# Loading 128 tokens' rows for all channels with one transfer, and the next head's v one slot later

## The chip, the cores and the metric

The kernel runs on one core of one Trainium2 chip. The metric is the device time of one execution in microseconds (us), taken as the median of several runs. A profile of one further execution (the profiled execution) shows each instruction of each engine: PE (matrix multiplications; PEld is its loading of weights), DVE (vector), ACT (activations), POOL (GpSimd) and SP, a queue that computes nothing and issues transfers (DMAs). In this kernel SP issues all of them, strictly in the order of the program: a transfer that has to wait for something holds up every later one.

## The reference

Causal attention with a decay over 8 batches x 8 heads of 576 tokens and 64 columns each, then a layer norm and a two-layer perceptron with a residual:

```python
B, H, S, D = q.shape                                   # 8, 8, 576, 64
scores = scale * np.matmul(q, k.transpose(0, 1, 3, 2))
cum = np.cumsum(np.log(np.clip(f, 0.0001, 1.0)), axis=-1)
scores = np.where(causal, -1000000000.0, scores + cum[:, :, :, None] - cum[:, :, None, :])
attn = np.exp(scores - np.max(scores, axis=-1, keepdims=True))
attn = attn / (np.sum(attn, axis=-1, keepdims=True) + 1e-09)
x = np.matmul(attn, v).transpose(0, 2, 1, 3).reshape(B, S, H * D)   # 8 x 576 x 512
mu, var = mean and variance of x over its last axis
xn = (x - mu) / np.sqrt(var + 1e-06) * g_ln
out = x + np.maximum(xn @ w_ch1, 0.0) @ w_ch2          # 512 -> 2048 -> 512
```

## The kernel before

**Heads and slots.** The 64 (batch, head) pairs are worked through one after the other. A head n has four query tiles t = 1 to 4 (a small tile 0 goes along with t = 1), and the program is a list of slots (n, t). The first 16 heads (`h.full`) run in one precision; from head 16 on (`NFULL`) operands are split in a high and a low part, and the scaled probabilities are carried from a tile `p` to a tile `pw` by a DMA (L440) before PE transposes them (L446). In slot (n, t) PE forms the scores (`qk_mm`, L376 and L377), DVE takes the maximum (L409), ACT the exponential (L420), DVE the reciprocal, POOL scales `p` (L427), and SP issues `pw<-p` (L440). The transposes of that tile are due two slots later (`LAG = 2`), the product with v (`av_unit`, L543) three slots later.

**The perceptron** takes chunks of 256 tokens and runs 16 steps per chunk (`FT`), one step in each slot as long as heads last, so that a chunk takes exactly four heads; what is left of it runs behind the last head. Before a chunk, its channels come back from DRAM (`xa`, `xb`: for each batch tokens 0 to 319 and 320 to 575) in four blocks of 128 channels, tiles `xr` (L655, `chunk_load`), which ACT and DVE split (L606, L607). For the layer norm's statistics and for the residual the same tokens are needed once more as rows: `rows_load` loads 128 tokens x 512 channels into a tile `xw`, again with channels on the partitions, and two steps later four PE transposes (`chunk_rows`, L446, `xp<-identr,xw`) turn it. `rows_load` runs in steps 9 and 11 of a chunk. In the part of the program where steps and slots go together, those are slots t = 1 and t = 3 of every fourth head, n = 17, 21, ..., 61.

**Order inside a slot.** A string of letters says which piece of which stage is written when. From slot 66 on it is

```python
    (66, "QSAFteahBlMPrmNbRLD"),
```

The letters that issue DMAs: `a` writes finished heads to `xa` or `xb` (L592), `B` issues `pw<-p`, `P` is `prep()` (a constant row `kl` at t = 2; the split of v, `prep_v`, at t = 3; `load_v` of the next head), `N` writes results, `R` loads `xw` and then `xr`, `D` loads a tile `raw` of q or k for the head after next (t = 2 and 3). Each engine works in the order in which the pieces are written. `prep_v` of head n reads the tile `vr` (DVE L356, then POOL L357), of which there is one buffer, so `load_v` of head n+1 (L332) has to wait for POOL L357 of head n.

**A wait behind each transfer.** Every DMA reports on one of eight semaphores, used in turn; a DMA also waits for the earlier one of its semaphore.

Of the kernel before, what the change touches and what calls it, by code (L numbers as in the profile page):

```python
# [8 lines left out]
F32 = mybir.dt.float32  # L9
# [6 lines left out]
B, H, S, D = 8, 8, 576, 64  # L16
DM, DFF = H * D, 4 * H * D
P = 128
KT = DM // P
FT = DFF // P  # L20
NTOK = B * S
C = 256
NCHUNK = NTOK // C
S1 = 320
# [4 lines left out]
LAG = 2  # L29
# [27 lines left out]
def attn_moe(ctx: ExitStack, tc: tile.TileContext, qk, v, f, g, w1, w2, out):  # L57
    nc = tc.nc
# [15 lines left out]
    def m2(name, dt):  # L74
        return work.tile([P, 512], dt, tag="m2", bufs=11, name=name)
# [8 lines left out]
    def busy(n):  # L84
# [9 lines left out]
        out=mask[:, S - P :], in_=mask[:, S - P :], pattern=[[-1, P]], base=0,  # L94
# [198 lines left out]
    xd1 = [dram.tile([DM, S1], F32, tag=f"xa{b}", name=f"xa{b}") for b in range(B)]  # L293
    xd2 = [dram.tile([DM, S - S1], F32, tag=f"xb{b}", name=f"xb{b}") for b in range(B)]
# [32 lines left out]
    def load_v(h):  # L327
        if h.full and h.n % 2 == 1:
            h.vr = work.tile([P, 5, 2, D], F32, tag="vv", bufs=1, name=f"vr{h.n}")[:, :, 0, :]
        else:  # L330
            h.vr = work.tile([P, 5, D], F32, tag="vr", bufs=1, name=f"vr{h.n}")
        nc.sync.dma_start(out=h.vr, in_=v[h.n])  # L332
# [28 lines left out]
    def qk_mm(h, t):  # L361
        q0, m, w = QT[t]
        cuts = [(0, w)] if w <= 512 else [(0, w // 2), (w // 2, w)]
        h.s = getattr(h, "s", {})
        h.s[t] = []
        if t == 0:
            w = P
            m = P if h.full else m
            cuts = [(0, w)]
        for i, (a, z) in enumerate(cuts):  # L370
            sp = bank(f"s{h.n}_{t}_{i}")[:m, : z - a]
            xq, kl = h.xq[:, q0 : q0 + m], h.kl[:, a:z]
            if h.full:
                mm(sp, xq, kl, start=True, stop=True)  # L374
            else:
                mm(sp, h.hi[:, 0, q0 : q0 + m], h.hi[:, 1, a:z], start=True, stop=False)  # L376
                mm(sp, xq, kl, start=False, stop=True)  # L377
            if t == 0:
                z, sp = a + QT[0][2], sp[: QT[0][1], : QT[0][2]]
            h.s[t].append((a, z, sp))  # L380
# [18 lines left out]
    def softmax_a(h, t):  # L399
        q0, m, w = QT[t]  # L400
        nm = f"{h.n}_{t}"
        if t == 0:
            pt = corner(h.n)
        else:
            pt = work.tile([P, S], F32, tag="p", bufs=3, name=f"p{nm}")
        st = work.tile([P, 4], F32, tag="st", bufs=6, name=f"st{nm}")
        off = S - P - (w - m)
        for i, (a, z, sp) in enumerate(h.s[t]):
            nc.vector.tensor_tensor_reduce(  # L409
                out=pt[:m, a:z], in0=sp, in1=mask[:m, off + a : off + z], scale=-SCALE,  # L410
                scalar=3.0e38 if i == 0 else st[:m, 0:1], op0=ALU.add, op1=ALU.min, accum_out=st[:m, i : i + 1],
            )
        h.p = getattr(h, "p", {})
        h.p[t] = (pt, st)

    def softmax_e(h, t):
        q0, m, w = QT[t]
        pt, st = h.p[t]
        i = len(h.s[t]) - 1
        nc.scalar.activation(pt[:m, :w], pt[:m, :w], AF.Exp, bias=st[:m, i : i + 1], scale=-1.0, accum_out=st[:m, 2:3])  # L420
# [81 lines left out]
    def transposed_hi(h, t):  # L502
        for tp, hi, lo in h.parts:
            nc.scalar.copy(out=hi, in_=tp)  # L504

    def transposed_lo(h):
        if not h.full:
            for tp, hi, lo in h.parts:
                nc.vector.tensor_tensor(out=lo, in0=tp, in1=hi.bitcast(F32), op=ALU.subtract)  # L509
# [129 lines left out]
    def mm2(c, j, h):  # L639
        if j == 0:  # L640
            c.acc = [ps.tile([P, DM], F32, tag=f"acc{i}", bufs=1, name=f"acc{c.n}_{i}") for i in range(2)]
        for i in range(2):
# [2 lines left out]
            mm(c.acc[i], h[:, 0, ts_], w2l[:, j, :], start=False, stop=False)  # L645
            mm(c.acc[i], h[:, 1, ts_], w2h[:, j, :], start=False, stop=(j == FT - 1))  # L646

    def tokens(c, k, t0, m, out_):

        t = t0  # L650
        while t < t0 + m:
            b, o = divmod(t, S)
            src, o0, lim = (xd1[b], 0, S1) if o < S1 else (xd2[b], S1, S)
            w = min(t0 + m - t, lim - o)
            nc.sync.dma_start(out=out_[:, t - t0 : t - t0 + w], in_=src[P * k : P * k + P, o - o0 : o - o0 + w])  # L655
            t += w

    def rows_load(c, i):
        c.xw = m2(f"xw{c.n}_{i}", F32R).rearrange("p (k c) -> p k c", k=KT)
        for k in range(KT):  # L660
            tokens(c, k, c.n * C + P * i, P, c.xw[:, k, :].bitcast(F32))

    def chunk_rows(c, i):

# [120 lines left out]
    hd = {}  # L785
# [14 lines left out]
    for u, slot in enumerate(slots):  # L800

        def before(k):
            return slots[u - k] if u >= k else None

        if slot is not None:
            n, t = slot
            h = hd[n]
        av = None
        if before(LAG + 1) is not None and before(LAG + 1)[1] in (2, 4):
            av = hd[before(LAG + 1)[0]]  # L810
        want = moe.can(wp.ready()) and u >= FIRST_MOE

        def piece(c):
            tu = before(LAG)
            if c == "t" and tu is not None:
                transpose_unit(hd[tu[0]], tu[1])
            elif c == "h" and tu is not None:
                transposed_hi(hd[tu[0]], tu[1])
            elif c == "l" and tu is not None:
                transposed_lo(hd[tu[0]])  # L820
            elif c == "Q" and slot is not None:
                if t == 1:
                    qk_mm(h, 0)
                qk_mm(h, t)
            elif c == "A" and av is not None:
                av_unit(av, before(LAG + 1)[1])
            elif c == "S" and slot is not None:
                if t == 1:
                    softmax_a(h, 0)
                softmax_a(h, t)  # L830
            elif c == "e" and slot is not None:
                if t == 1:
                    softmax_e(h, 0)
                softmax_e(h, t)
            elif c in FILL:
                wp.fill(FILL[c])
            elif c == "s":
                wp.sums()
                if u == LAG:
                    busy(WARM[2])  # L840
            elif c == "F" and av is not None:
                finish(av)
            elif c == "a" and av is not None:
                finish_add(av)
            elif c == "r" and want:
                moe.first_high()
            elif c == "R":
                moe.limit = min(NCHUNK, max(0, u - LAG - 1) // (4 * H) * S // C)
                moe.rest()
            elif c == "b":  # L850
                rows_stats(moe.cur)
            elif c == "L":
                run_later(RSTD)
            elif c == "M" and want:
                moe.first()
            elif c == "B" and slot is not None:
                if t == 1:
                    softmax_b(h, 0)
                softmax_b(h, t)
            elif c == "m" and want:  # L860
                moe.first_low()
            elif c == "W":
                due = 1 + min(u, W_CHANGE) / W_SLOTS + max(0, u - W_CHANGE) * W_TICKS
                while not wp.done() and wp.tick_no <= due:
                    wp.tick()
            elif c == "N":
                moe.second()
            elif c == "P":
                prep()
            elif c == "D":  # L870
                next_raw()

        def next_raw():

            if slot is not None and t in (2, 3) and NFULL <= n + 2 < B * H:
                if t == 2:
                    start_head(n + 2)
                load_raw(hd[n + 2], 1 if t == 2 else 0)

        def prep():  # L880

            if slot is not None:
                if t == 1 and n + 1 < NFULL:
                    start_head(n + 1)
                if n == NFULL - 2 and t == 1:
                    while not wp.done():
                        wp.tick()
                        wp.fill(99)
                    early.close()
                    pools["late"] = ctx.enter_context(tc.tile_pool(name="late", bufs=1))  # L890
                if n + 1 >= NFULL and n + 1 < B * H:
                    if t == 2:
                        prep_a(hd[n + 1])
                    if t == 3:
                        prep_b(hd[n + 1])
                if not h.full and t == LAG + 1:
                    prep_v(h)
                if t == LAG + 1 and n + 1 < B * H:
                    load_v(hd[n + 1])

        for c in [o for first, o in ORDERS if first <= u][-1]:
            piece(c)
# [48 lines left out]
```

## Time and profile before

| | |
|---|---|
| time, median of 3 runs | 1250.09 us (1249.48 to 1256.52) |
| profiled execution | 1250.83 us, its span from first to last instruction 1249.1 us |
| PE busy | 1197.9 us of the span, 96% |
| DVE, ACT, POOL busy | 749.0, 620.4, 452.4 us |
| DMA | 139.04 MB in 129657 packets, mean 111 GB/s |
| mean granted clock of PE | 0.990 |

Three stages follow each other: the full heads with the unpacking of the weights (to 223 us), the heads 16 to 63 with the perceptron's steps (223 to some 1030 us), and the rest of the perceptron (to 1249 us). Busy time counts instructions that compute. "Idle before, releaser" at a row is how long its engine had nothing to do, and what ended that.

### The profile page before, as it was taken

How to read it: one execution, taken by the hardware profiler on the slowest of the kernel's cores; microseconds unless marked ns; L12 is line 12 of the kernel's file. 1: busy time of each engine (PE TensorE's matmuls, PEld its weight loads, DVE VectorE, ACT ScalarE, POOL GpSimd, SP SyncE). 2: the span in 40 equal slices, each digit the busy share in tenths (PEclk: the TensorE clock that was granted, in tenths of full speed). 3: DMA queues.
4: the chain of work that ended last, by engine and by line, in shares of the span. 5: the costliest groups of instructions: out<-in, count | busy, mean ns of one | idle time of the engine just before them, and what ended most of it. 6: DMA issues, size and time to landing. Idle time of an engine off the chain costs nothing.

```text
span 1249.1 us, 26052 instructions
## 1 busy us (share of the span) xinstructions
PE 1197.9 (96%) x8368; PEld 1070.7 (86%) x8368; DVE 749.0 (60%) x2664; ACT 620.4 (50%) x1936; POOL 452.4 (36%) x768
## 2 busy tenths in 40 slices
PE   8888998999999999999999999998989999999998
PEld 6557887889898989899898989887989899999997
DVE  6777683466676767676666676766767662222222
ACT  6886574455555555555455555555545542112111
POOL 3544344344444434354434444444434330000000
PEclk9998998999999999999999999999999999999999
DMA  6554442244334343433433444433343421110100
GB/s 187 150 158 144 128 133 66 87 131 130 116 128 140 124 136 125 137 125 117 134 124 126 131 133 131 133 121 116 127 130 124 137 81 39 51 35 17 52 27 26
DMA packets 129657, 139.04 MB, mean 111 GB/s; under 512 B 34544, under 2 KB 102128, under 8 KB 129520
## 3 DMA queue, kind: packets, MB, share of 16 engines
q1 hardware_dynamic: 129520, 137.37, 35.6%
q8 instruction: 67, 1.10, 0.4%
q14 instruction: 70, 0.57, 0.2%
HBM read 79.61 MB, written 19.17 MB: 79 GB/s over the span
## 4 chain that ended last, share of the span: by engine, by line
PE 81%; DVE 6%; DMA 5%; ACT 4%; issue 2%; POOL 1%; SPq 1%; DVEq 0%; POOLq 0%; ACTq 0%
PE h L622 11%; PE h L624 10%; PE h L623 10%; PE acc L644 10%; PE acc L645 10%; PE acc L646 10%; PE o L543 5%; DMA pw<-p 4%; PE tr L446 4%; PE s L376 3%; PE s L377 3%; PE s L374 2%; PE o L518 2%; DVE p L409 2%; ACT p L420 2%
## 5 line engine op out<-in xcount | busy, mean ns | idle before, releaser
L427 POOL TENSOR_SCALAR p<-p,st 64x64 f32<-64x64 f32 (+4 forms) x320 | 169.7, 532 | 542.2 <-ACT ph L504 310.0
L622 PE MATMUL h<-x,w1h 128*128 128x256 f32 x1152 | 342.3, 297 | 5.7 <-DVE pl L509 5.3
L624 PE MATMUL h<-x,w1l 128*128 128x256 f32 x1152 | 326.8, 284 | 0.0
L623 PE MATMUL h<-x,w1h 128*128 128x256 f32 x1152 | 326.4, 283 | 0.0
L420 ACT ACTIVATE p<-p,st 64x64 f32<-64x64 f32 (+4 forms) x320 | 179.2, 560 | 229.0 <-DVE st L409 216.6
L635 DVE SCALAR_TENSOR_TENSOR hh<-h,hh 128x256 fp32r<-128x256 f32 x288 | 120.4, 418 | 194.9 <-ACT hh L630 194.8
L622 PEld LDWEIGHTS h<-x,w1h 128*128 128x128 f32 x1152 | 219.6, 191 | 11.0 <-issue 6.6
L644 PE MATMUL acc<-w2h,hh 128*128 128x512 f32 x576 | 228.9, 397 | 0.0
L645 PE MATMUL acc<-w2l,hh 128*128 128x512 f32 x576 | 228.3, 396 | 0.0
L646 PE MATMUL acc<-w2h,hh 128*128 128x512 f32 x576 | 225.9, 392 | 0.0
L623 PEld LDWEIGHTS h<-x,w1h 128*128 128x128 f32 x1152 | 220.9, 192 | 2.5
L624 PEld LDWEIGHTS h<-x,w1l 128*128 128x128 f32 x1152 | 220.6, 191 | 0.0
L630 ACT ACTIVATE hh<-h 128x256 fp32r<-128x256 f32 x288 | 109.9, 382 | 185.0 <-PE h L624 184.6
L409 DVE CUSTOM_DVE_ANT_0 p<-s,mask 64x64 f32<-64x64 f32 (+4 forms) x320 | 132.4, 422 | 43.8 <-DMA pw<-p 22.1
L646 PEld LDWEIGHTS acc<-w2h,hh 128*128 128x128 f32 x576 | 108.7, 189 | 25.0
L644 PEld LDWEIGHTS acc<-w2h,hh 128*128 128x128 f32 x576 | 109.9, 191 | 14.2 <-ACT ph_full L504 0.2
L425 DVE TENSOR_SCALAR st<-st 128x1 f32<-128x1 f32 (+1 forms) x320 | 47.5, 149 | 121.0 <-ACT p L420 118.2
L645 PEld LDWEIGHTS acc<-w2l,hh 128*128 128x128 f32 x576 | 109.8, 191 | 11.9
L504 ACT CAST ph<-tr 64x128 fp32r<-64x128 f32 (+4 forms) x384 | 107.2, 328 | 3.7 <-PE tr L446 1.4
L579 ACT COPY ot<-o 64x320 f32<-64x320 f32 x96 | 37.9, 395 | 119.3 <-PE tr L446 60.1
L446 PE MATMUL tr<-identr,pw 128*128 128x128 f32 (+1 forms) x672 | 79.4, 235 | 18.3 <-DMA pw<-p 18.2
L509 DVE TENSOR_TENSOR pl<-tr,ph 128x128 fp32r<-128x128 f32 x192 | 88.0, 458 | 4.4
(89 smaller groups left out, 1885.1 us busy)
## 6 DMA issues: line engine op xcount, KB each, us to landing
raw<-in_qk_dram SPq DMA_DIRECT2D x96, 288.0 KB, 2.9
wr<-in_w_dram SPq DMA_DIRECT2D x32, 512.0 KB, 5.9
pw<-p SPq DMA_DIRECT2D x48, 288.0 KB, 3.3
pw<-p SPq DMA_DIRECT2D x48, 224.0 KB, 2.2
vr<-in_v_dram SPq DMA_DIRECT2D x64, 160.0 KB, 2.3
out_dram<-xt SPq DMA_DIRECT2D x36, 256.0 KB, 2.1
pw<-p SPq DMA_DIRECT2D x48, 160.0 KB, 2.1
xa<-xs SPq DMA_DIRECT2D x32, 160.0 KB, 1.8
```

The source lines that it names most:

```text
L409: nc.vector.tensor_tensor_reduce(out=pt[:m, a:z], in0=sp, in1=mask[:m, off + a : off + z], scale=-SCALE, scalar=3.0e38 if i == 0 else st[: ...
L420: nc.scalar.activation(pt[:m, :w], pt[:m, :w], AF.Exp, bias=st[:m, i : i + 1], scale=-1.0, accum_out=st[:m, 2:3])
L427: nc.gpsimd.tensor_scalar(out=pt[:m, :w], in0=pt[:m, :w], scalar1=st[:m, 3:4], scalar2=1.0, op0=ALU.mult, op1=ALU.mult)
L446: nc.tensor.transpose(out_.bitcast(F32R), in_, identr[:m, :m])
L622: mm(ph, w1h[:, k, fs], c.x[k][:, 0, :], start=(k == 0), stop=False)
L623: mm(ph, w1h[:, k, fs], c.x[k][:, 1, :], start=False, stop=False)
L624: mm(ph, w1l[:, k, fs], c.x[k][:, 0, :], start=False, stop=(k == KT - 1))
L630: nc.scalar.activation(h[:, 0, :], c.ph, AF.Relu)
L635: nc.vector.scalar_tensor_tensor(out=h[:, 1, :], in0=ph, scalar=0.0, in1=h[:, 0, :].bitcast(F32), op0=ALU.max, op1=ALU.subtract)
L644: mm(c.acc[i], h[:, 0, ts_], w2h[:, j, :], start=(j == 0), stop=False)
L645: mm(c.acc[i], h[:, 0, ts_], w2l[:, j, :], start=False, stop=False)
L646: mm(c.acc[i], h[:, 1, ts_], w2h[:, j, :], start=False, stop=(j == FT - 1))
```

## The change

Two edits. `rows_load` issues one DMA for all four blocks of 128 channels instead of one DMA per block: the source is viewed as partition x block x token. Where the 128 tokens lie on both sides of a border between `xa` and `xb`, there are two such DMAs, in place of eight. In all, 44 DMAs write `xw` instead of 176. And for heads that aren't full, `load_v` of the next head is issued at t = 4 instead of t = 3.

```diff
+    def piece_of(t, end):
+        b, o = divmod(t, S)
+        src, o0, lim = (xd1[b], 0, S1) if o < S1 else (xd2[b], S1, S)
+        return src, o - o0, min(end - t, lim - o)
...
     def rows_load(c, i):
         c.xw = m2(f"xw{c.n}_{i}", F32R).rearrange("p (k c) -> p k c", k=KT)
-        for k in range(KT):
-            tokens(c, k, c.n * C + P * i, P, c.xw[:, k, :].bitcast(F32))
+        t = t0 = c.n * C + P * i
+        while t < t0 + P:
+            src, o, w = piece_of(t, t0 + P)
+            nc.sync.dma_start(
+                out=c.xw[:, :, t - t0 : t - t0 + w].bitcast(F32),
+                in_=src.rearrange("(k p) s -> p k s", p=P)[:, :, o : o + w],
+            )
+            t += w
...
-                if t == LAG + 1 and n + 1 < B * H:
+                if t == LAG + 1 and h.full and n + 1 < B * H:
+                    load_v(hd[n + 1])
+                if t == LAG + 2 and not h.full and n + 1 < B * H:
                     load_v(hd[n + 1])
```

`tokens`, which loads `xr`, uses `piece_of` too and does what it did. PE, DVE, ACT and POOL keep their instructions in their order; what moves is on SP.

The first place is SP around slot (17, 3). In a row, `pw17_3` is head 17's tile 3, `vr18` is v of head 18, `xw1_1` the second half of chunk 1's rows, `xr2_3` a block of chunk 2. Before:

```order
L440 DMA pw17_3_3249<-p17_3_3220 128x448
L332 DMA vr18_3272<-in_v_dram 128x320
L655 DMA xw1_1_3288<-xb0_155 128x128 x4
L655 DMA xr2_3_3293<-xb0_155 128x64
L655 DMA xr2_3_3293<-xa1_148 128x192
L325 DMA raw19_0_3296<-in_qk_dram 128x576
L440 DMA pw17_4_3318<-p17_4_3304 128x576
L592 DMA xa2_149<-xs16_0_3094 128x320
```

And with the change (lines from L646 on have other numbers there):

```order
L440 DMA pw17_3_3237<-p17_3_3208 128x448
L666 DMA xw1_1_3274<-xb0_155 128x4x128
L658 DMA xr2_3_3276<-xb0_155 128x64
L658 DMA xr2_3_3276<-xa1_148 128x192
L325 DMA raw19_0_3279<-in_qk_dram 128x576
L440 DMA pw17_4_3301<-p17_4_3287 128x576
L332 DMA vr18_3318<-in_v_dram 128x320
L592 DMA xa2_149<-xs16_0_3088 128x320
```

Between `pw17_3` and `pw17_4` stood seven DMAs, the wait of `vr18` ahead of the others; now there are four, and `vr18` stands behind `pw17_4`.

The second place is SP from slot (17, 1) on, where the rows cross a border. Before:

```order
L440 DMA pw17_1_3116<-p17_1_3085 128x192
L655 DMA xw1_0_3142<-xa0_147 128x64
L655 DMA xw1_0_3142<-xb0_155 128x64
L655 DMA xw1_0_3142<-xa0_147 128x64
L655 DMA xw1_0_3142<-xb0_155 128x64
L655 DMA xw1_0_3142<-xa0_147 128x64
L655 DMA xw1_0_3142<-xb0_155 128x64
L655 DMA xw1_0_3142<-xa0_147 128x64
L655 DMA xw1_0_3142<-xb0_155 128x64
L655 DMA xr2_1_3154<-xb0_155 128x64
L655 DMA xr2_1_3154<-xa1_148 128x192
L440 DMA pw17_2_3177<-p17_2_3160 128x320
```

And with the change:

```order
L440 DMA pw17_1_3110<-p17_1_3079 128x192
L666 DMA xw1_0_3136<-xa0_147 128x4x64
L666 DMA xw1_0_3136<-xb0_155 128x4x64
L658 DMA xr2_1_3142<-xb0_155 128x64
L658 DMA xr2_1_3142<-xa1_148 128x192
L440 DMA pw17_2_3165<-p17_2_3148 128x320
```

Ahead of `xr2_1` and `pw17_2` stood eight DMAs, and now two.

More of the change, by code (lines that the diff above doesn't have):

```diff
@@ L651, in tokens @@
         while t < t0 + m:
[L652 to L655, printed above, removed]
+            src, o, w = piece_of(t, t0 + m)
+            nc.sync.dma_start(out=out_[:, t - t0 : t - t0 + w], in_=src[P * k : P * k + P, o : o + w])
             t += w
```

## The prediction

> **What bounds the kernel now.** I read the profile from coarse to fine: busy time by stage, PE's waits, the lengths of heads, and then the queue SP at the places where PE waits. First busy time, in the stage of heads 16 to 63 and the stage behind it. The columns are the stretch, its length, busy time (and instructions) of PE, PEld, DVE, ACT and POOL, granted clock, DMA share and GB/s.
>
> ```profile
> 223.40:1006.10 782.70, 757.25 (x5415) 694.20 (x5414) 526.95 (x1937) 420.51 (x1337) 339.48 (x539) 1.00 0.40 126
> 1006.10:1249.10 243.00, 239.14 (x1559) 216.84 (x1557) 69.18 (x176) 50.00 (x141) 19.58 (x85) 1.00 0.13 40
> ```
>
> PE is the bound in both. In the last stage 3.9 us of 243 are not PE's, and no transfer of this change can give more there. In the stage of heads 25 us are missing, and no other engine is near its limit: PE stands still at single places. Whom it waits for there (us in total, times, longest):
>
> ```profile
> PE tr L446 <- DMA pw<-p: 18.2, 14, 2.6
> PE h L622 <- DVE pl L509: 5.3, 4, 1.3
> PE o L543 <- DVE ph L509: 1.5, 4, 0.4
> ```
>
> What a stall costs in all is seen in the length of heads. Each row is the first matmul of a head, and its first column the start: heads 16, 17, 33, 34, 35, 36 and 63.
>
> ```profile
> 223.43 0.22 PE L376 MATMUL s<-hi 128*64 128x128 f32 x1
> 240.24 0.22 PE L376 MATMUL s<-hi 128*64 128x128 f32 x1
> ...
> 505.56 0.22 PE L376 MATMUL s<-hi 128*64 128x128 f32 x1
> 521.68 0.22 PE L376 MATMUL s<-hi 128*64 128x128 f32 x1
> 542.07 0.22 PE L376 MATMUL s<-hi 128*64 128x128 f32 x1
> 557.82 0.22 PE L376 MATMUL s<-hi 128*64 128x128 f32 x1
> ...
> 1007.61 0.22 PE L376 MATMUL s<-hi 128*64 128x128 f32 x1
> ```
>
> Head 35 takes 15.75 us and has no stall. Head 33 has none either, but four transposes of rows: 16.12. Head 34, the next one, has the same work and takes 20.39. So a chunk's first and fourth head cost 15.75 and its second and third 16.12 where PE never waits. The 47 heads from 223.43 to 1007.61 take 784.18 us; without waits they would take 24 x 16.12 + 23 x 15.75 = 749.13. **35.05 us are lost**. Of these, 1.06 are head 16's (16.81 against 15.75), in which no `xw` is loaded, and 0.62 + 0.44 belong to two waits in slots where none is issued either:
>
> ```profile
> 644.92 0.47 PE L446 MATMUL tr<-identr,pw 128*64 128x128 f32 x4 [0.62 <-DMA pw<-p]
> ...
> 826.15 0.39 PE L446 MATMUL tr<-identr,pw 128*64 128x128 f32 x3 [0.44 <-DMA pw<-p]
> ```
>
> That leaves 35.05 - 2.12 = 32.9 us for sixteen places: slot t = 3 of the twelve heads 17, 21, ... 61, and slot t = 1 of four of these. Part of it is clock. The first row is the stretch that holds head 34's wait, the others two stretches right behind waits (head 34's and head 42's), with the granted clock third from the end of the row:
>
> ```profile
> 527.34:530.75 3.41, 1.60 (x15) 1.63 (x16) 0.82 (x4) 1.04 (x4) 0.00 (x0) 1.00 0.51 182
> 530.75:534.17 3.42, 3.42 (x11) 2.84 (x11) 2.34 (x6) 1.69 (x5) 2.47 (x5) 0.50 0.18 58
> 663.87:667.28 3.41, 3.41 (x15) 3.12 (x14) 2.03 (x7) 2.54 (x8) 1.94 (x2) 0.50 0.14 49
> ```
>
> Half the clock for 3.41 us costs 1.7 us each time, 3.4 in all.
>
> **Slot t = 3, both edits.** Head 17's, on SP, then what POOL did, then PE's wait:
>
> ```profile
> 254.88 0.47 SPq L440 DMA_DIRECT2D pw<-p  x1
> 257.49 0.33 SPq L332 DMA_DIRECT2D vr<-in_v_dram  x1
> 257.88 1.85 SPq L655 DMA_DIRECT2D xw<-xb  x4
> ...
> 261.26 0.47 SPq L440 DMA_DIRECT2D pw<-p  x1
> 261.82 0.54 SPq L592 DMA_DIRECT2D xa<-xs  x1
> ```
>
> ```profile
> 254.94 1.57 POOL L350 TENSOR_TENSOR hi<-raw,hi 64x576 fp32r<-64x576 f32 x1
> 256.58 0.88 POOL L357 TENSOR_TENSOR vv<-vr,vv 128x320 fp32r<-128x320 f32 x1
> 258.48 0.74 POOL L427 TENSOR_SCALAR p<-p,st 128x576 f32<-128x576 f32 x1 [1.02 <-ACT ph L504]
> ```
>
> ```profile
> 264.68 0.48 PE L446 MATMUL tr<-identr,pw 128*64 128x128 f32 x4 [1.27 <-DMA pw<-p]
> ```
>
> SP was free at 255.35, but the load of v stood first in line until POOL L357 ended (256.58 + 0.88 = 257.46). Behind it came four `xw`, two `xr` and `raw`, and only then tile 4's `pw`. Its probabilities were ready at 258.48 + 0.74 = 259.22, and it left at 261.26: 2.04 us late, for which PE then waited 1.27.
>
> With the change SP issues one `xw` at 255.35, two `xr` (0.43 each), and `raw` as soon as POOL L350 has read its buffer (256.51) and is through at 256.9. Then it waits for the probabilities, so that `pw` leaves at 259.2. What does the merged issue cost? Nearest rows: the weights' load in the same form (four blocks to a partition), and one block (ns min/median/max).
>
> ```profile
> L150 SPq DMA_DIRECT2D wr<-in_w_dram x16: 379/384/592, 2.6 to 167.9; - x16
> ```
>
> ```profile
> L655 SPq DMA_DIRECT2D xw<-xa x96: 319/430/583, 149.4 to 1179.4; - x96
> ```
>
> So 0.38 if blocks are free, 4 x 0.43 = 1.72 if each is paid for. I take 0.43. Here it makes no difference: at 1.72 SP is through at about 258.3, still ahead of 259.2. All twelve places go.
>
> Landing times (KB each, us from issue to landing) of what is merged, moved and waited for:
>
> ```profile
> wr<-in_w_dram SPq DMA_DIRECT2D x32, 512.0 KB, 5.9
> pw<-p SPq DMA_DIRECT2D x48, 288.0 KB, 3.3
> ```
>
> ```profile
> vr<-in_v_dram SPq DMA_DIRECT2D x64, 160.0 KB, 2.3
> ```
>
> `pw` then lands at 259.2 + 3.3 = 262.5; PE could have come to it at 264.68 - 1.27 = 263.4. 0.9 us to spare, so that the wait goes whole. A merged `xw` of 256 KB lands between 0 and 3.9 us later than four of 64 KB: the upper end gives it the 5.9 of 512 KB. It is due two slots later, 2 x 15.75 / 4 = 7.9 us, so I put its cost at nothing. v moves one slot (3.9 us) nearer to its use three slots on, with a landing of 2.3: nothing. Its issue of 0.33 us now stands behind `pw`, where SP is idle.
>
> **Slot t = 1, the merged load alone.** In four heads (17, 21, 53, 57) eight `xw` stand there, each issued in some 0.43 us, ahead of a block `xr`. Head 17's, on SP the last of that block, then ACT and PE:
>
> ```profile
> 249.28 0.43 SPq L655 DMA_DIRECT2D xr<-xa  x1
> ```
>
> ```profile
> 251.47 0.41 ACT L606 CAST x<-xr 128x256 fp32r<-128x256 f32 x1 [3.41 <-DMA xr<-xa]
> ```
>
> ```profile
> 255.00 0.36 PE L622 MATMUL h<-x,w1h 128*128 128x256 f32 x1 [1.32 <-DVE pl L509]
> ```
>
> ACT stood 3.41 us for a block `xr` that was queued behind eight `xw`; what ACT and DVE owed PE came 1.32 us late, and 0.38 more a slot later. Six issues fewer take 6 x 0.43 = 2.6 us off the queue, more than 1.32: both go. If each block is paid for, nothing changes here, and 5.3 + 1.5 = 6.8 us stay.
>
> **The sum.** 12 places at t = 3 and 4 at t = 1: -32.9 us on the profiled execution, 1250.83 - 32.9 = **1218 us** (its median of three is 1250.09, 0.06% lower). A smaller sum has only PE's idle time and the clock: 18.2 - 1.06 + 5.3 + 1.5 + 3.4 = 27.3, or 1223. I take the heads' lengths, since they also hold the refilling of PE behind a stall.
>
> **The rivals.** (1) *The issue costs by block.* Then t = 1 stays as it is: 1218 + 6.8 = **1225**. For it: one-block issues all take about 0.43. Against: 384 ns for the four-block row. The Trainium skill (DMA: Bandwidth & Descriptors, "Issuing engines are not separate DMA queues") says that time to initiate a DMA on a sequencer "is usually small relative to the DMA itself". By that, merging would bring nothing, and it would be 1225 too; the rows above differ, with a queue of eight issues that held ACT for 3.41 us.
>
> (2) *The slow clock isn't the stalls'.* If the two stretches at 0.50 come anyway, 3.4 us stay: **1221**. For it: most stalls have no such stretch behind them. Against: both lie right behind a wait, and a stretch with PE busy for 1.60 of 3.41 us precedes the first. The Trainium skill (TensorE: Matmul & The Clock Gate, "What's actually happening") has the clock drop after an idle window of about 3.4 us; PE's longest wait here is 2.6, so by its rule these waits drop nothing and 1221 would be the time. The trace doesn't agree: the clock fell behind a window that was 47% busy.
>
> (3) *Slower: v now competes with tile 4's `pw`.* It used to leave ahead of it; now it follows in 47 heads, also in those that never wait. The fourth tile of a head that didn't wait (head 32) shows the room, from SP's issue to PE's use:
>
> ```profile
> 505.88 0.47 SPq L440 DMA_DIRECT2D pw<-p  x1
> ```
>
> ```profile
> 509.95 0.46 PE L446 MATMUL tr<-identr,pw 128*64 128x128 f32 x4
> ```
>
> 4.07 us, less 3.3 for the landing: 0.8. If v's 160 KB delay `pw` by x, 47 x (x - 0.8) is lost; it turns the gain over from x = 1.5, and at its own landing time, x = 2.3, it is 70 us: 1218 + 70 = **1288**. Against: at 261.82 in the rows above, 160 KB of `xa` follow `pw` just so, and such a `pw` still needs 3.3.
>
> (4) *SP isn't what holds `pw`.* Then the time stays, **1250**. For it: POOL's rows show a wait for ACT as well. Against: the probabilities were ready 2.04 us before `pw` left.
>
> **How the numbers follow.** My forecast, 1218, has 0.66; (1) 0.09; (2) 0.12; (3) 0.08, of which half ends below 1237 and 0.03 above 1263; (4) 0.05. The range: down to 1212, if the 2.1 us that I left out go as well, with some scatter; up to 1230, over 1225 and the smaller sum, with a fifth of the twelve places left as they are (5 us). A measurement of this kernel tells about 1% from no change. Faster by more than that: 0.66 + 0.09 + 0.12 + 0.04 = 0.91; within it: 0.05 + 0.01 = 0.06; slower: 0.03.
>
> **What would show it.** In the profile after, heads 18, 22, ... take 16.1 us, the waits of PE's L446 for `pw` fall from 18.2 to 1 or 2 us, and no load of v waits for POOL L357 on SP. An `xw` issue of 0.4 us speaks for the forecast at t = 1, one of 1.7 for (1). A clock of 0.50 between 223 and 1200 us would be (2). New waits for `pw` at tile 4 in heads 19, 20, 23, 24 would be (3), and the forecast would be wrong by the number of heads.

## The result and the profile after

The changed kernel takes 1215.22 us (median of 4 runs, 1213.07 to 1217.98) against 1252.36 us for the kernel before in the same series (1249.48 to 1256.52): a ratio of **0.970, 95% interval 0.966 to 0.974**. Its profiled execution took 1217.98 us with a span of 1216.1, so that profile against profile the change brought 1250.83 - 1217.98 = 32.85 us. By the medians it is 37.1 us: the profiled execution is the slowest of the four.

The four runs of after scatter by 5 us in the order of their mean granted clocks (0.993, 0.994, 0.997, 0.998 from slowest to fastest); in the profiled one, stretches at half clock lie in the first 200 us, near 97, 104 and 193 us as in the profile of before.

Busy time in the stage of heads and in the stage behind it, kernel after (columns as before: stretch, length, PE, PEld, DVE, ACT, POOL, granted clock, DMA share, GB/s):

```profile
223.40:974.40 751.00, 750.78 (x5423) 692.54 (x5422) 535.96 (x1942) 421.24 (x1343) 340.89 (x545) 1.00 0.42 132
974.40:1216.10 241.70, 237.69 (x1551) 215.71 (x1549) 68.19 (x173) 48.34 (x135) 18.41 (x79) 1.00 0.13 40
```

The first stage shrank from 782.7 to 751.0 us, and PE now lacks 0.2 us in it instead of 25. The second stage kept its 4 us. PE's waits between 223.4 and 980 us, all that are left (us in total, times, longest):

```profile
PE o L543 <- DVE ph L509: 0.2, 1, 0.2
```

The three rows of before, 18.2 + 5.3 + 1.5 us, are gone. The starts of heads 16, 17, 33, 34, 35, 36 and 62:

```profile
223.47 0.22 PE L376 MATMUL s<-hi 128*64 128x128 f32 x1
240.27 0.22 PE L376 MATMUL s<-hi 128*64 128x128 f32 x1
...
495.88 0.22 PE L376 MATMUL s<-hi 128*64 128x128 f32 x1
512.00 0.22 PE L376 MATMUL s<-hi 128*64 128x128 f32 x1
528.11 0.22 PE L376 MATMUL s<-hi 128*64 128x128 f32 x1
543.86 0.22 PE L376 MATMUL s<-hi 128*64 128x128 f32 x1
...
958.24 0.22 PE L376 MATMUL s<-hi 128*64 128x128 f32 x1
```

Head 34 takes 528.11 - 512.00 = 16.11 us, where it took 20.39. Heads 33 and 35 keep their 16.12 and 15.75. With head 62's 16.11 the 47 heads take 958.24 + 16.11 - 223.47 = 750.88 us, 33.3 less than before and 1.75 above the 749.13 of heads that never wait. The stage ahead of them (223.4 us) did not move.

On SP, the two waits that changed most are that for the buffer of v, first row, kernel before:

```profile
SPq L332 <- POOL vv L357: 71.9, 35, 2.2
```

and, in the kernel after, those that SP has instead:

```profile
SPq L440 <- POOL p L427: 290.5, 179, 10.7
...
SPq L325 <- POOL hi L350: 37.3, 35, 1.1
```

v never waits for POOL L357 any more. The time in which SP stood for it went to waits that hurt nobody: 228.4 us for the probabilities became 290.5 (SP is early and waits for POOL, as it should be), and the load of `raw` now waits for its own buffer. SP around slot (17, 3), kernel after:

```profile
252.61 0.47 SPq L440 DMA_DIRECT2D pw<-p  x1
253.13 0.59 SPq L666 DMA_DIRECT2D xw<-xb  x1
253.82 0.52 SPq L658 DMA_DIRECT2D xr<-xb  x1
254.39 0.42 SPq L658 DMA_DIRECT2D xr<-xa  x1
254.92 0.37 SPq L325 DMA_DIRECT2D raw<-in_qk_dram  x1
257.03 0.47 SPq L440 DMA_DIRECT2D pw<-p  x1
257.56 0.58 SPq L332 DMA_DIRECT2D vr<-in_v_dram  x1
```

Four transfers stand between the two `pw`, where there were eight (v, four `xw`, two `xr` and `raw`). One `xw`, two `xr` and `raw` are through at 255.3. Then SP stands idle until the probabilities are ready; POOL and PE in the same place:

```profile
256.26 0.75 POOL L427 TENSOR_SCALAR p<-p,st 128x576 f32<-128x576 f32 x1 [1.06 <-DMA xw<-xb]
```

```profile
261.14 0.46 PE L446 MATMUL tr<-identr,pw 128*64 128x128 f32 x4
```

POOL ends at 257.01 and `pw` leaves 0.02 us later, where it was 2.04 us late. PE's transpose has no bracket behind it: it didn't wait. (POOL waited 1.06 us, as it did 1.02 for ACT in before; that its bracket now names an `xw` tells only which event came last by the profile.) From issue to use there are 261.14 - 257.03 = 4.11 us; by the semaphore records `pw` landed after 2.52, so 1.6 us were to spare.

Two things got better there, by the same records. At the twelve places of t = 3 `pw` had left 1.5 to 3.8 us late and then taken 3.0 to 4.0 us to land (medians 2.06 and 3.3). Now it leaves at once and lands after 2.4 to 3.5 us (median 2.46), as it does in the other heads (2.48 now, 2.47 before). `raw`, the transfer of 288 KB right ahead of it, left 0.4 to 0.6 us before it at eleven of the twelve places, and leaves 1.8 to 3.1 us before it at eleven of them now (0.9 us in head 61, where `pw` takes 3.3 us to land).

At slot t = 1, ACT's wait for the block `xr` in head 17 and, for all heads, ACT's waits for `xr`; kernel after:

```profile
249.04 0.41 ACT L606 CAST x<-xr 128x256 fp32r<-128x256 f32 x1 [0.50 <-DMA xr<-xa]
```

```profile
ACT x L606 <- DMA xr<-xa: 7.7, 8, 1.7
ACT x L606 <- DMA xr<-xb: 7.1, 6, 2.3
```

and before, for all heads:

```profile
ACT x L606 <- DMA xr<-xa: 17.7, 13, 3.4
ACT x L606 <- DMA xr<-xb: 16.7, 10, 4.3
```

3.41 us became 0.50 in head 17, and the sum of ACT's waits fell from 34.4 to 14.8.

### The profile page after: what moved, and what is told of

The parts are those of the page before. It is cut to its first block, busy times and chain, and to the rows that moved or that the text cites. A ratio compares the mean times of both kernels' runs of the same rounds, so it can differ in the third digit from the quotient of the medians.

```text
span 1216.1 us, 25716 instructions
## 1 busy us (share of the span) xinstructions
PE 1190.1 (98%) x8368; PEld 1068.3 (88%) x8368; DVE 757.0 (62%) x2664; ACT 619.3 (51%) x1936; POOL 452.6 (37%) x768
## 4 chain that ended last, share of the span: by engine, by line
PE 91%; DVE 3%; ACT 2%; DMA 1%; issue 1%; POOL 1%; SPq 0%; DVEq 0%; ACTq 0%; POOLq 0%
PE h L622 12%; PE h L624 11%; PE h L623 11%; PE acc L644 11%; PE acc L645 11%; PE acc L646 11%; PE o L543 6%; PE tr L446 4%; PE s L376 3%; PE s L377 3%; PE s L374 2%; PE o L518 2%; PE tr L448 1%; ACT p L420 1%; DVE p L409 1%
## 5 line engine op out<-in xcount | busy, mean ns | idle before, releaser
L644 PE MATMUL acc<-w2h,hh 128*128 128x512 f32 x576 | 228.4, 397 | 0.0
L646 PE MATMUL acc<-w2h,hh 128*128 128x512 f32 x576 | 225.5, 391 | 0.0
L646 PEld LDWEIGHTS acc<-w2h,hh 128*128 128x128 f32 x576 | 108.5, 188 | 24.7
L377 PE MATMUL s<-kl,xq 66*128 66x288 f32 (+4 forms) x288 | 83.2, 297 | 0.0
```

Of the source, the lines that this page charges most:

```text
L644: mm(c.acc[i], h[:, 0, ts_], w2h[:, j, :], start=(j == 0), stop=False)
```

## The experiments

Two questions were open: which edit does what, and how near the new order is to its limit. The first four kernels shared a chip with the kernel before at 1248.92 us (1243.86 to 1254.1, 7 runs), the last four another one with it at 1253.28 (1248.43 to 1256.11, 7 runs). "Lost" below is the length of the 47 heads over 749.13 us in the profile: 35.05 before, 1.75 after. It tells the kernels apart better than the time does, since the stage ahead of these heads, in which little differs between them, took 218.4 to 228.0 us in the ten profiles, with 3.4 to 30.7 us of it at half clock.

### Merged loads alone

```diff
-                if t == LAG + 1 and h.full and n + 1 < B * H:
-                    load_v(hd[n + 1])
-                if t == LAG + 2 and not h.full and n + 1 < B * H:
+                if t == LAG + 1 and n + 1 < B * H:
                     load_v(hd[n + 1])
```

> The merged load of xw alone; the load of v stays at t = 3 and waits for POOL L357 there. Theory A (PE waits only where SP lets go of pw or xr too late, and a lateness below PE's spare time of 0.9 to 1.2 us costs nothing): in head 17 v goes at 257.5, then xw 0.58, two xr 0.9, raw 0.4, so that pw leaves 0.5 to 0.7 us after its probabilities (1.1 where xw crosses a border), inside the spare time. So nearly the whole gain: 1215 to 1220 us, heads 18, 22, ... at 16.1 to 16.4 us. Theory B (each edit takes away its own share of the lateness and of the time): the wait of 2.05 us behind v is half of what was in front of pw, so half of the 26 us of the places at t = 3 comes back: about 1228.

Measured: 1221.33 us (1218.84 to 1223.55), ratio 0.977 [0.973, 0.982], 1.3 us above theory A's range and well below B's 1228. 7.7 us are lost. PE's waits in the stage of heads:

```profile
PE tr L446 <- DMA pw<-p: 5.3, 7, 2.2
```

Both rows of t = 1 are gone, so they were the eight issues' alone. At t = 3 most of the loss is gone too, though v is still in front (head 34 loses 1.3 us instead of 4.3): with three issues fewer behind it, `pw` leaves 0.0 to 1.4 us late (median 0.2). But the reserve is used up, and by the landing: with `xw`, two `xr` and `raw` sent right ahead of it, `pw` takes 3.7 to 5.8 us to land at the twelve places (median 4.0, by the semaphore records), where it took 3.3 before and takes 2.5 after. The dearest of the seven waits, in head 54: SP, then PE, then the packets by queue from that issue on.

```profile
828.01 0.33 SPq L332 DMA_DIRECT2D vr<-in_v_dram  x1
828.40 0.43 SPq L666 DMA_DIRECT2D xw<-xb  x1
828.88 0.50 SPq L658 DMA_DIRECT2D xr<-xb  x1
829.42 0.43 SPq L658 DMA_DIRECT2D xr<-xa  x1
829.95 0.38 SPq L325 DMA_DIRECT2D raw<-in_qk_dram  x1
830.43 0.47 SPq L440 DMA_DIRECT2D pw<-p  x1
```

```profile
836.38 0.48 PE L446 MATMUL tr<-identr,pw 128*64 128x128 f32 x4 [2.21 <-DMA pw<-p]
```

```profile
q8 instruction: 1, 0.02, 1.6%
```

This `pw` took 5.8 us to land by the semaphore records, and a packet of the instruction queue fell into it (more on that below). In after, `pw` has 1.0 to 2.0 us to spare in 38 of the 48 heads, and most late landings pass unseen.

### v late alone

The same edit to `load_v` as in the change, with `rows_load` as before:

```diff
-                if t == LAG + 1 and n + 1 < B * H:
+                if t == LAG + 1 and h.full and n + 1 < B * H:
+                    load_v(hd[n + 1])
+                if t == LAG + 2 and not h.full and n + 1 < B * H:
                     load_v(hd[n + 1])
```

> The load of v at t = 4 alone; xw in one DMA per block as before. Theory A: at t = 3 SP starts the four or eight xw 2 us earlier and is through about when the probabilities are ready (up to 1.2 us late with eight), so the places at t = 3 cost nothing; the four places at t = 1 (heads 17, 21, 53, 57 at 17.7 to 18.1 us instead of 16.1, and 0.4 in the head behind each) stay, 9 us: 1224 to 1227 us. Theory B: the share of v alone, half of 26 us: about 1237.

Measured: 1230.49 us (1227.99 to 1236.18), ratio 0.985 [0.980, 0.989]; 12.1 us lost. The time lies between theory A (1224 to 1227) and B (1237).

```profile
PE h L622 <- DVE pl L509: 5.3, 4, 1.3
PE o L543 <- DVE ph L509: 1.5, 4, 0.4
PE tr L446 <- DMA pw<-p: 0.8, 1, 0.8
```

The rows of t = 1 are those of before to the digit, at the same four heads (17, 21, 53 and 57 take 17.65 to 17.86, the heads behind them 16.71 to 16.85). At t = 3 the four issues of `xw` are still in the queue, and yet only one of the twelve places makes PE wait by more than 0.15 us: head 37's, where eight stand. The heads speak for A: of the 12.1 us, 9.05 are those of t = 1, for which A had 9, and 1.06 are head 16's; A put the other 2 us at nothing.

So t = 1 belongs to the merge, and t = 3 to both: either edit takes most of that loss away. Hence the single gains, 2.3% and 1.5%, sum to more than the 3.0% of the two together. The heads show it more clearly: 27.4 us less are lost with the merge alone and 23.0 with the later v alone, and 33.3 with both. (The times alone do not tell the merge from both edits: the interval 0.973 to 0.982 overlaps with 0.966 to 0.974.)

### Many small issues

The changed kernel with each `xw` split into eight issues everywhere (by block and half of the partitions, or by block and side of the border):

```diff
-            nc.sync.dma_start(
-                out=c.xw[:, :, t - t0 : t - t0 + w].bitcast(F32),
-                in_=src.rearrange("(k p) s -> p k s", p=P)[:, :, o : o + w],
-            )
+            for k in range(KT):
+                for p0 in range(0, P, P if w < P else 64):
+                    p1 = p0 + (P if w < P else 64)
+                    nc.sync.dma_start(
+                        out=c.xw[p0:p1, k, t - t0 : t - t0 + w].bitcast(F32),
+                        in_=src[P * k + p0 : P * k + p1, o : o + w],
+                    )
```

> The changed kernel with its xw in eight DMAs at every load: one for each block and each half of the partitions (where a border is crossed, each block and each side of it). Same bytes, same runs of 512 bytes where no border is crossed, 288 issues instead of 44. Theory A (issues on SP): all twelve heads 17, 21, ... lose at t = 1 what four of them lost before, 1.8 us and 0.4 in the head behind, 26 us; at t = 3 pw is some 1.2 us late against a spare time of 0.9 to 1.2, 0 to 4 us in all. 1241 to 1247 us. Theory C (the merged transfer helps as a transfer, by bytes or landing, not by fewer issues): no difference, 1213 to 1218 us.

Measured: 1289.31 us (1284.97 to 1292.67), ratio 1.031 [1.027, 1.035]; 70.2 us lost. PE's waits, then the issues of `xw` (ns min/median/max, first and last start):

```profile
PE tr L446 <- DMA pw<-p: 18.7, 13, 2.7
PE h L622 <- DVE pl L509: 14.9, 12, 1.3
PE s L376 <- DVE st L409: 5.4, 7, 1.1
```

```profile
L669 SPq DMA_DIRECT2D xw<-xa x160: 376/594/1533, 153.1 to 1221.9; - x160
L669 SPq DMA_DIRECT2D xw<-xb x128: 319/594/1327, 252.6 to 1261.8; - x128
```

The same bytes in more issues lose more than before did, so the price is that of the issue. That issues don't matter (the theory that expected 1213 to 1218) fell. The theory of the queue was right in the direction, and far too low (1241 to 1247), for two reasons that the trace names. An issue of 64 partitions isn't cheaper than one of 128 but dearer, 0.594 us against 0.43 in the same run, so that `pw` leaves 1.2 to 4.1 us late at the twelve t = 3 places (median 2.9) and PE waits at eleven of them, and at all twelve t = 1 places PE waits, for 1.2 us in the mean. And 13 stretches of 3.4 us at half clock lie in the stage of heads, 22 us, where before had two.

### More bytes behind `pw`

The changed kernel with 288 KB more, DRAM to DRAM, issued right behind `load_v` in each head from 16 on:

```diff
                 if t == LAG + 2 and not h.full and n + 1 < B * H:
                     load_v(hd[n + 1])
+                    extra = dram.tile([P, S], F32, tag="extra", bufs=1, name=f"extra{n}")
+                    nc.sync.dma_start(out=extra, in_=qk[n][:, 0, :])
```

> The changed kernel with 288 KB more behind tile 4's pw in each of the heads 16 to 62: right behind the load of v, a copy of q and k rows from DRAM to a scratch in DRAM that nobody reads. Theory A (transfers of one queue go through the rings in order, what follows hardly delays what is ahead): 1214 to 1219 us, landing of tile 4's pw as in the changed kernel (2.4 to 2.5 us in most heads). Theory D (rival 3 of the prediction: what follows pw takes its share): pw lands up to 2.9 us later, against a spare time of 1.2 to 1.7 us, and 47 heads lose up to 1.3 us or so: up to 1275 us.

Measured: 1225.63 us (1221.62 to 1233.47), ratio 0.981 [0.976, 0.986]; 13.8 us lost. PE's waits, and ACT's for `xr`:

```profile
PE o L543 <- DVE ph L509: 4.6, 7, 1.7
PE tr L446 <- DMA pw<-p: 1.3, 3, 0.7
```

```profile
ACT x L606 <- DMA xr<-xa: 17.6, 7, 3.8
ACT x L606 <- DMA xr<-xb: 13.3, 5, 3.8
```

If what follows `pw` slowed it much, 448 KB behind it in 47 heads would (that theory expected up to 1275). `pw` of tile 4 lands after 2.48 us in the median, as in after; at the twelve places of t = 3 it is 2.8 against 2.5. What became late is the transfer that follows the extra bytes: ACT's waits for `xr` are back from 14.8 to 30.9 us. So the sum of the theory that held for `pw` (1214 to 1219) was short by some 7 us, and the delay that the third rival feared from v (up to 2.3 us for each `pw`) is refuted with more bytes than v has.

### The change again, with tile 4's `pw` held up

The second series runs the changed kernel again, beside two that issue small copies (64 KB of the same probabilities) just ahead of tile 4's `pw`, two in one and four in the other (`range(4 ...)`):

> The changed kernel once more, beside the three others of this set. 1212 to 1219 us, ratio to before 0.966 to 0.976; against the merged load alone (0.977) it should be lower by about 5 us, as the heads' lengths had it in the profiles.

Measured for the change: 1217.55 us (1214.56 to 1222.58), ratio 0.973 [0.969, 0.977], 3.0 us lost.

```diff
+            for j in range(2 if t == 4 else 0):
+                late = dram.tile([P, P], F32, tag=f"late{j}", bufs=1, name=f"late{h.n}_{j}")
+                nc.sync.dma_start(out=late, in_=pt[:, 0:P])
             nc.sync.dma_start(out=pw[:m, :w].bitcast(F32), in_=pt[:m, :w])
```

> The changed kernel with two small copies (64 KB of the same probabilities, DRAM scratch that nobody reads) issued just ahead of tile 4's pw in all heads from 16 on: pw leaves some 1.0 us later in 48 heads. Theory A (lateness inside PE's spare time is free): spare time is 1.0 us in the heads 18, 22, ... and 1.5 in the others, so 0 to 0.2 us in twelve heads and some more waits where a transfer lands late: 1215 to 1223 us. Theory B (lateness costs in proportion; before, 27 us of lateness at twelve places went with 26 us lost there): 48 us more, 1263 us.

> The same with four copies: pw leaves some 2.0 us later in 48 heads, above the spare time. Theory A: 0.5 us lost in 36 heads and 1.0 in twelve, 30 us, and perhaps some of the slow clock behind them: 1243 to 1255 us. Theory B: 96 us more, about 1311 us. If nothing were lost (1215 to 1220 us), SP's lateness would not be what PE waited for at all.

Measured: with two copies 1229.55 us (1227.38 to 1234.75), ratio 0.982 [0.978, 0.986], 14.3 us lost; with four 1265.26 us (1263.38 to 1273.59), ratio 1.011 [1.007, 1.016], 47.6 us lost. PE's waits with two:

```profile
PE tr L449 <- DMA pw<-p: 6.1, 8, 1.7
```

and with four, with SP and PE in head 34:

```profile
PE tr L449 <- DMA pw<-p: 28.3, 37, 1.9
```

```profile
543.41 1.74 SPq L442 DMA_DIRECT2D late<-p  x4
545.26 0.47 SPq L443 DMA_DIRECT2D pw<-p  x1
```

```profile
547.85 0.48 PE L449 MATMUL tr<-identr,pw 128*64 128x128 f32 x4 [0.73 <-DMA pw<-p]
```

This is the reserve, measured. Two copies make `pw` 0.9 us late and leave about half of the heads at their clean lengths; four make it 1.87 late (543.38, when POOL is done, to 545.26), and nearly every head waits. Where the four copies run smoothly, heads take 0.3 to 0.85 us more (heads 45 to 48 together 66.18 against 63.74), while PE's waits among them are 0.1 to 0.7: these short waits, 1.38 us in four heads, cost 2.44, or 1.8 times their length. (The longer ones of before cost 1.23 times theirs: 32.9 less 3.4 for the clock, by 18.2 - 1.06 + 5.3 + 1.5 = 23.9 us.) So the spare time lies between 0.9 and 1.9 us, and the 2.04 us of before were beyond it. Theory A had the shape, and its upper ends (1223 and 1255) were passed by 7 and 10 us. The surplus sits in groups of neighbouring heads. SP in head 39 of the run with four copies, and the packets of the instruction queue while one of these copies was issued:

```profile
626.80 3.44 SPq L442 DMA_DIRECT2D late<-p  x4
```

```profile
q8 instruction: 1, 0.02, 4.7%
```

The four copies took 3.44 us here, against 1.74 in head 34, since the issue of one took 2.12 instead of 0.42. The same holds for the heads 25 to 28, 38 to 40 and 50 to 53, where one issue took 1.0 to 2.1 us and `pw` left 2.4 to 3.6 us late. The earlier transfer of that copy's semaphore had landed at least 3.4 us before, so it was not what SP waited for. With two copies, such issues (heads 26, 38, 50 and 51) and landings of 3.1 to 4.0 us fall into heads 25 to 27, 38 to 40 and 49 to 53. That lateness costs in proportion in every head (1263 and 1311) fell.

### A version tried for more time

What is left in the stage of heads is under 2 us, so the last kernel tried to spend the freed time in the stage ahead of it, by taking up the unpacking of the weights sooner:

```diff
-W_SLOTS, W_CHANGE, W_TICKS = 2.4, 34, 0.8
+W_SLOTS, W_CHANGE, W_TICKS = 2.4, 34, 1.0
```

> The changed kernel with the unpacking of the weights at 1.0 instead of 0.8 pieces per slot from slot 34 on. What is left of PE's waits in the changed kernel is in the first stage; the longest, 3.2 us at 193.7 us with 6.8 us at half the clock behind it, is POOL's scaling of p behind four pieces of weights that are unpacked at once when head 14 starts. Spread over the slots before, they should cost nothing there: 6.6 us less, 1208 to 1212 us. Rival: DVE and ACT are at 60 to 70% in those slots, and the pieces only bring the same wait forward: 1213 to 1219 us.

Measured: 1219.42 us (1218.25 to 1221.08), ratio 0.974 [0.971, 0.976], not to be told from the change's 0.973. The 1208 to 1212 that were hoped for did not come.

```profile
PE o L543 <- DVE ph L509: 3.9, 4, 1.4
```

A wait of 3.2 us near 193 us went, but the perceptron's steps then stand otherwise against the slots, a chunk's first head takes 16.05 us instead of 15.75, these waits come, and the 47 heads lose 9.0 us. No version better than the change was found.

## Why the prediction was right

**The sum** said 32.9 us less in the profiled execution, and 32.85 were measured; 1218 us stand against a median of 1215.22, inside 1212 to 1230. That the two differences agree to 0.05 us is luck: the four runs of after scatter by 5 us, and by the medians 37.1 us were gained. What the sum was made of, the length of the 47 heads, shrank by 33.3 us (by 32.1 in the profile of the change's second run). Its terms one by one:

- *The sixteen places.* All are clean, heads 18, 22, ... 62 at 16.11 to 16.18 (but for head 30, 16.33, behind a wait of 0.2 us), so the length of heads, not PE's idle time (27.3, 1223 us), was the right measure. The four-copy run shows it again: a head loses more than its wait.
- *The 2.12 us set aside.* The sum said that they stay. 1.06 did: head 16 takes 16.81 still. The waits of 0.62 and 0.44 went, and new losses of 0.7 came in heads 29 and 30. This step was wrong in its reason: these waits weren't tied to a place in the program but to two `pw` that took 4.7 and 4.6 us to land, see below.
- *The issue.* I took 0.43 us for four blocks, with bounds of 0.38 and 1.72. The 44 issues of after have a median of 0.58, since most stand right behind a `pw`, where issues of a single block took 0.58 too in before (kernel after):

```profile
L666 SPq DMA_DIRECT2D xw<-xa x24: 370/582/1912, 149.4 to 1144.7; - x24
L666 SPq DMA_DIRECT2D xw<-xb x20: 373/583/1297, 244.9 to 1184.7; - x20
```

  With v ahead of it instead, as in the run of the merge alone, it is 0.43 (the row at 828.40). Rival (1), a price per block, has fallen: four blocks cost what one costs in the same place, a third of the 1.72. With it fell the application of the Trainium skill's sentence (DMA: Bandwidth & Descriptors, "Issuing engines are not separate DMA queues") to this kernel. An issue is small against its transfer, 0.4 to 0.6 against 2.4 us, as that sentence says; but with eight in a row ahead of it, ACT waited 3.41 us for a block `xr`.
- *The merged transfer's landing,* put at nothing, cost nothing: 256 KB land after 3.1 us in the median, against 2.0 for 64 KB before, and are due 7.9 us later.
- *The spare time.* 0.9 us was predicted for head 17's tile 4, from a landing of 3.3, before and after. 3.3 was right for the twelve places before (median 3.3; 2.5 in the other heads), but the landing did not stay: it fell to 2.46, so that `pw` has 1.4 to 2.0 us to spare at ten of the twelve places (0.4 and 1.2 where it landed after 3.5 and 3.3). That the row of before says 3.3 is luck, too. It is the median of 7 of the 48, those of the one semaphore whose records are complete; the page of after, where none is complete, gives no landing in the same row.

```profile
pw<-p SPq DMA_DIRECT2D x48, 288.0 KB
```

  The median of all 48 was 2.76 before. The step that took the landing as given was wrong, on the safe side: the time did not hang on it.
- *Rival (2), clock.* In after's clock records no stretch at half clock lies between 223 and 1200 us. The two of before came behind stretches with PE busy for 47% and 62%, and where the stalls went, the 3.4 us went with them.
- *Rival (3), v behind `pw`.* No head waits at tile 4. 448 KB behind `pw` left its landing at 2.48 us in the median.
- *Rival (4), SP isn't the holder.* `pw` left 0.02 us after the probabilities.

What the prediction did not see is that **the two edits overlap**. It gave t = 3 to "both edits" and never asked for each alone: merging alone brings 2.3%, the later v alone 1.5%. Of the change's 3.0%, v's later load adds only what is left of t = 3, 5 to 6 us by the lengths of heads (7.7 us lost against 1.75, and 3.0 in the second run).

## What to carry to other kernels

Where one queue issues all transfers in order, count the issues and the waits between the moment when a transfer could leave and the moment when it does: here 0.4 to 0.6 us for each issue, whatever it carries, and some 2 us for a load that stood first in line for its buffer. Look also at what is sent right ahead of the transfer that matters: `pw` landed after 2.5 us where little was, and after 4.0 right behind `xw`, `xr` and `raw`. Put a load whose buffer comes free late behind the transfer that the bound engine needs next, and let one issue carry many blocks. Measure the reserve that is left (here 0.9 to 1.9 us) by delaying that transfer on purpose: a kernel just inside it, as the merge alone, pays for each transfer that lands late by chance.

## What the runs showed of the hardware

**Beside instruction packets, transfers land late and issues are slow.** Packets of 16 KB of the instruction queue (q8) come every 17 to 19 us in the stage of heads, 67 in an execution, and each takes 0.9 to 2.1 us. Sorted by whether one fell into the 2.6 us behind the issue, the landings of tile 3's `pw` (224 KB, seldom with anything ahead of it) are, worked out from the packet and semaphore records:

```
kernel             without: number, median, over 3.0 us     with: number, median, longest, over 3.0 us
before                      38      2.22    0                     10      2.94    4.45     5
after                       39      2.21    0                      9      2.66    4.35     2
merged loads alone          39      2.22    0                      9      2.57    4.12     3
v late alone                38      2.22    0                     10      3.00    4.16     5
weights sooner              38      2.22    4                     10      3.85    4.35     9
all ten profiles           389              4                     91                     41
```

Without such a packet a landing of more than 3 us hardly occurs (4 of 389, all in the run with the weights sooner); with one it is 41 of 91. The two waits that the prediction set aside and the 5.8 us in head 54 of the merge alone each have such a packet. SP's issues show it more sharply: of the 8793 issues in the ten traces 175 took more than 0.9 us, and during 172 of these such a packet was under way, against 425 of the other 8618. The slow issues of copies in the delayed runs are among them. No run changed the program's length or its fetching, so this is a correlation and not an experiment.

**Half clock needs no idle window.** Over all ten traces, from the start of head 16 to the end of head 63, the windows of 3.41 us at full clock in which PE was busy for less than 53% were followed by one at half clock in 11 of 12 cases; between 53% and 66% it was 5 of 27; above that, none. The Trainium skill (TensorE: Matmul & The Clock Gate, "What's actually happening") speaks of an idle window of about 3.4 us; none here was idle for more than 61%. So a stall of 2 us can cost 1.7 us more, and the run with many small issues paid that 13 times. Why some windows around 60% drop the clock and others don't stays open.

**An issue of half the partitions is dearer than a whole one:** 0.594 us for 64 partitions (32 KB) against 0.43 for 128 (64 KB, or 256 KB in four blocks, where no `pw` stands right ahead), on the same queue.
